# adaLN attention and gated FFN on one core: VectorE sums the softmax denominators over eight key tiles instead of two

## The chip, the core and the metric

The kernel runs on one core of a Trainium2 chip. Five engines work side by side, each through its own instruction stream in order: TensorE (PE, with its weight loads shown as PEld), VectorE (DVE), ScalarE (ACT), GpSimd (POOL) and SyncE (SP), whose only work here is issuing DMA transfers. They wait for each other through semaphores. The metric is the device time of one execution in microseconds (us); the kernel before takes 1217.15 us, the median of three runs from 1216.24 to 1217.86.

## The reference

`x` has 2048 tokens of width 1024. Six modulation vectors come from `silu(c) @ w_mod`. Then, in bf16:

```
h = layernorm(x) * (1 + ca) + sa
q = h @ wq (32 heads of 32);  k = h @ wk, v = h @ wv (one shared head of 32)
p = softmax(q k^T / sqrt(32));  o = p @ v;  x = x + ga * (o @ wo)
h = layernorm(x) * (1 + cb) + sb
x = x + gb * ((silu(h @ w1) * (h @ w3)) @ w2)          # inner width 3584
```

The softmax needs, for each query and head, the sum of its 2048 exponentials. How those sums are made is the core of the change.

## The kernel before

**Tiling.** Queries go in 8 blocks of 256 tokens (`n`). The 32 heads go in 8 groups of 4 (`f`); a block and a group are a *unit* (64 units). A unit runs over 2048 keys in 8 *cycles* (`j`) of two key tiles of 128 keys. So there are 512 cycles.

**One cycle** (`s_exp`): eight score matmuls S (four heads side by side in the array's 32-row strips) write two pairs of the six score banks of PSUM. ScalarE takes two exponentials of 128x1024 from them into `U[c % 10]`. VectorE then adds the two key tiles of the cycle (`pair`, 128x1024, bf16) into `PS[c % 8]`.

**The end of a unit** (`av`): after the unit's last exponential, TensorE runs eight value groups A (eight matmuls each, `V` against `U`, into the left half of one PSUM bank), and after every second one a denominator group M: `ONES` against two of the pair sums `PS`, eight matmuls, into the right half of the same bank. That is four M groups in a unit, 256 in the kernel. Then VectorE normalises: a 32x32 transpose of the right half into `RB[:,0]`, a reciprocal of eight columns, a transpose back into `RB[:,1]`, and a multiply of the bank's left half by it into `QT`. The bank is held until that multiply.

**The rest of a block**: `wo` (output projection, added to `X1` on VectorE, layer norm, transposes), `slab` (14 FFN slabs: gate into one bank, up into another; VectorE halves the gate, ScalarE takes a tanh, VectorE combines, then multiplies with the up bank), `quarter` (four quarters of the down projection; VectorE scales with `GBR`, POOL adds to `X1`). The FFN of block n runs in between the attention of block n+1; the last one runs alone at the end. W1, W3 and W2 are read again for each block, through three slab buffers and two quarter buffers, by SP.

**Banks.** Six of the eight PSUM banks belong to the scores; only two (`PB`) are left for all value, projection and FFN work until the last exponentials are done.

**What sets the order.** A planner (`Placer`) writes each engine's stream at build time. It is a list scheduler: each operation has a duration that the code states, and a `vt` (a due time in cycles). On each engine the operation that can start first goes first, and among those that can start about then the one with the lowest `vt`. On TensorE, S has the lowest (`TOP + c`), then A and M (`-500 + u`), then FFN and projections; a change of the array's mode costs `SWITCH`, and a change between A and F work soon after an S is put off (`HOLD`). On VectorE pair sums have `c + 100`, behind everything else. A TensorE operation of the planner is a group of matmuls that is not split: four in `slab`, `wo` and `q_proj`, seven in `quarter`. `emit` adds the semaphore waits; a VectorE instruction waits for an earlier VectorE instruction only where it reads or overwrites what that one wrote.

All instructions are issued through one helper (`play`, line 22), so the profile names them by tile, not by line. `PB<-PS,ONES` are the M groups, `PB<-U,V` the A groups, `S<-QT,KT` the scores, `PB<-QT,W` and `PB<-QT,HT` the slabs, `PB<-W2S,HT` the quarters. `HT` names all FFN intermediates, which lie in the space of `HT`.

Of the kernel before, what the change touches and what calls it, by code (L numbers as in the profile page):

```python
# [111 lines left out]
class Placer:  # L112

    SWITCH = 0.098
# [114 lines left out]
    def commit(self, n, e, k, start):  # L229
# [11 lines left out]
        if e == "sp" or n.dma is not None:  # L241
            self.t[e] = start + dur
            self.bw = max(self.bw, start + 1.6) + n.nbytes / n.bw
            n.fin = self.bw + 0.5
        else:
            self.t[e] = start + dur
            n.fin = start + dur + n.post + self.SEM
# [24 lines left out]
    def emit(self, n, e, fn):  # L272
# [8 lines left out]
        for p, strong in sorted(n.preds.items(), key=lambda a: -a[0].i):  # L281
            if p.eng == e and p.dma is None and (e == "pe" or not strong):
                continue
# [68 lines left out]
def build(nc, x_in, wq_in, wk_in, wv_in, wo_in, w1_in, w3_in, w2_in, c_in, wmod_in, out, S, D, F):  # L352
# [164 lines left out]
    def ln_stats(xap, tt, keys, vt):  # L517
        for a in range(2):
            op("dve", lambda a=a: [lambda e: e.bn_stats(ST[:, tt, a, :], xap[:, a * 512:(a + 1) * 512])], 0.64,
               reads=keys, writes=[("ST", tt, a)], vt=vt)  # L520
        op("dve", lambda: [lambda e: e.bn_aggr(MV[:, tt, :], ST[:, tt, :, :].rearrange("p a f -> p (a f)"))], 0.17,
# [6 lines left out]
    def ln_norm(xap, tt, keys, slot, vt):  # L528
        op("dve", lambda: [lambda e: e.tensor_scalar(XN[slot], xap, MV[:, tt, 0:1], RS[:, tt:tt + 1],
                                                     ALU.subtract, ALU.mult)], 0.52,  # L530
           reads=keys + [("MV", tt), ("RS", tt)], writes=[("XN", slot)], vt=vt)

    def lnt1(tt, vt):
# [3 lines left out]
        if tt < 8:  # L537
# [4 lines left out]
                                                      scale=RS[:, tt:tt + 1])], 0.98,  # L542
# [11 lines left out]
        op("pe", tr, 0.95, reads=[("XN", slot), "IDENT"], writes=bk, vt=vt, mode="F", sess=s, post=0.2)  # L554
# [8 lines left out]
        op("act", ev_a, 0.98, reads=bk, writes=hk, vt=vt, sess=s, alts=[("dve", ev_d, 0.72)])  # L563

    def mod_cols(fld):
        s = Sess()
        for h in range(2):
# [4 lines left out]
               writes=[("mod", fld)], vt=-1800, mode="F", sess=s, post=0.2)  # L572
# [20 lines left out]
    def k_bias():  # L593
# [4 lines left out]
           sess=s3, post=0.2)  # L598
# [3 lines left out]
    def v_setup():  # L602
# [5 lines left out]
           0.4, reads=["SABR", ("WKV", 1)], writes=["vbr"], vt=-1290, mode="F", sess=s, post=0.2)  # L608
# [3 lines left out]
    def q_bias(f0, f1, key, vt):  # L612
# [4 lines left out]
           reads=[key, "SAB"], writes=[("qbi", f0)], vt=vt, mode="F", sess=s, post=0.2)  # L617
# [3 lines left out]
    def k_proj(j, vt):  # L621
# [6 lines left out]
           writes=[("k", j)], vt=vt, mode="F", sess=s, post=0.2)  # L628
        op("dve", lambda b: [lambda e: e.tensor_scalar(KT[:, ts], BANK[b][:, 0:256], KBI[:, 0:1], None, ALU.add)],
           0.45, reads=[("k", j), "KBI"], writes=[("KT", j)], vt=vt, sess=s,  # L630
           alts=[("act", lambda b: [lambda e: e.activation(KT[:, ts], BANK[b][:, 0:256], ACT.Identity,
                                                           bias=KBI[:, 0:1])], 0.45)])

    def v_proj(tb, vt):
        s = Sess()
        hk = [("HT", cc, tt) for cc in range(NC) for tt in range(4 * tb, 4 * tb + 4)]
        for k in range(4):
# [4 lines left out]
               mode="F", sess=s, post=0.2)  # L642
        op("dve", lambda b: [lambda e: e.tensor_tensor(
            V[:, 4 * tb:4 * tb + 4, :], BANK[b][:, 0:128].rearrange("p (k d) -> p k d", d=32),
            VBR[:].unsqueeze(1).broadcast_to([P, 4, 32]), ALU.add)], 0.3, reads=[("v", tb), "VBR"],
           writes=[("V", tb)], vt=vt, sess=s)

    def q_proj(n, nn, f, vt, cold=1.0):
# [6 lines left out]
        for h in range(2):  # L655
# [3 lines left out]
                for cc in range(4 * h, 4 * h + 4)], pe_mm(w, 4) * cold, reads=wk + hk, writes=[("q", n, f)], vt=vt,  # L659
               mode="F", sess=s, post=0.2)  # L660
        op("dve", lambda b: [lambda e: e.tensor_scalar(
            QT[:, n:n + nn, f, :], BANK[b][:, 0:w].rearrange("p (a t) -> p a t", a=nn), QBI[:, f:f + 1], None,
            ALU.add)], 0.2 + 0.28 * nn, reads=[("q", n, f), ("QBI", f)],
# [4 lines left out]
    def mod_chunk(i, vt):  # L668
# [3 lines left out]
        if i == 1:  # L672
# [7 lines left out]
           writes=[("mc", i)], vt=vt, mode="F", sess=s, post=0.2)  # L680
        if fld in (2, 5):
            op("dve", lambda b: [lambda e: e.tensor_copy(MG[:], BANK[b][:, 0:4])], 0.17, reads=[("mc", i)],
               writes=["MG"], vt=vt, sess=s)
            for k in range(4):
# [5 lines left out]
               reads=["ONES", ("XN", 1)], writes=[("mct", i)], vt=vt, mode="F", sess=s2, post=0.2)  # L690
# [15 lines left out]
    def s_exp(c):  # L706
# [9 lines left out]
        op("pe", mm, 0.225, reads=[("KT", j), ("QT", n, f)], writes=bk, vt=TOP + c, mode="S", post=0.18)  # L716
        for i in range(2):
            def ex(i=i):
# [3 lines left out]
            exps[(c, i)] = op("act", ex, 0.93, reads=[("S", 2 * r[i]), ("S", 2 * r[i] + 1)],  # L722
                              writes=[("U", c % NU, i)], vt=c, post=0.09)

    def pair(c):
        op("dve", lambda: [lambda e: e.tensor_tensor(PS[:, c % NP], U[:, c % NU, :, 0, :], U[:, c % NU, :, 1, :],
                                                     ALU.add)], 0.64,
           reads=[("U", c % NU, 0), ("U", c % NU, 1)], writes=[("PS", c % NP)], vt=c + 100.0)

    def av(u):  # L730
        n, f = u // NC, u % NC
        s = Sess(False)
        for q in range(NP):
            pair(u * NJ + q)
        for q in range(NJ):
            def mm(b, q=q):
# [5 lines left out]
               writes=[("av", u)], vt=-500 + u, mode="A", sess=s, post=0.2, after=[exps[(u * NJ + LAG, 1)]])  # L742
            if q % 2:
                def md(b, q=q):
                    return [lambda e, h=h, k=k: e.matmul(
                        BANK[b][32 * h:32 * (h + 1), B:2 * B], ONES[:, 0:32], PS[:, (u * NJ + k) % NP, h, :],
                        start=False, stop=(k == NJ - 1), tile_position=(0, 32 * h), skip_group_check=True)
                        for k in (q - 1, q) for h in range(4)]
                op("pe", md, 0.22, reads=["ONES"] + [("PS", (u * NJ + k) % NP) for k in (q - 1, q)],
                   writes=[("av", u)], vt=-500 + u, mode="A", sess=s, post=0.2)  # L750
                for k in (q + NP - 1, q + NP):
                    if k < NJ:
                        pair(u * NJ + k)
        vt = u * 8.0
        op("dve", lambda b: [lambda e: e.transpose(RB[:, 0, :], BANK[b][:, B:2 * B])], 0.4, reads=[("av", u)],
           writes=["RBD"], vt=vt, sess=s)
        op("dve", lambda: [lambda e: e.reciprocal(RC[:], RB[:, 0, :].rearrange("p (a r) -> p a r", r=32)[:, :, 0])],
           0.2, reads=["RBD"], writes=["RC"], vt=vt)
        op("dve", lambda: [lambda e: e.transpose(RB[:, 1, :].rearrange("p (a r) -> p a r", r=32),
                                                 RC[:].unsqueeze(2).broadcast_to([P, 8, 32]))], 0.4,  # L760
           reads=["RC"], writes=["RBN"], vt=vt)
        op("dve", lambda b: [lambda e: e.tensor_tensor(QT[:, n, f, :], BANK[b][:, 0:B], RB[:, 1, :], ALU.mult)], 0.42,
           reads=[("av", u), "RBN"], writes=[("QT", n, f)], vt=vt, sess=s)
# [10 lines left out]
    def wo(n, vt):  # L774
        for t in range(2):
            for h in range(2):
                s = Sess()
                for q in range(2):
                    op("pe", lambda b, q=q, h=h, t=t: [lambda e, f=f: e.matmul(
                        BANK[b], QT[:, n, f, t * P:(t + 1) * P], WO[:, f, h * 512:(h + 1) * 512], start=(f == 0),  # L780
                        stop=(f == NC - 1)) for f in range(4 * q, 4 * q + 4)], pe_mm(512, 4),
                       reads=[("QT", n, f) for f in range(4 * q, 4 * q + 4)] + [("WOG", f) for f in
                                                                                 range(4 * q, 4 * q + 4)],
                       writes=[("wo", n, t, h)], vt=vt, mode="F", sess=s, post=0.2)
                xs = X1[:, n % NX, t, h * 512:(h + 1) * 512]
                k = xk(n, t, (2 * h, 2 * h + 1))
                op("dve", lambda b, xs=xs: [lambda e: e.tensor_tensor(xs, xs, BANK[b], ALU.add)], 0.7,
# [3 lines left out]
        for hh in range(2):  # L791
# [4 lines left out]
               writes=[("h2", n, hh)], vt=vt, mode="F", sess=s, post=0.2)  # L796
            for k in range(4):
# [3 lines left out]
                    ALU.mult, ALU.add)], 0.42,  # L801
# [17 lines left out]
    def slab(n, s, vt):  # L819
# [4 lines left out]
        for m in range(2):  # L824
            for sub in range(2):
                for c0 in (0, 4):
                    op("pe", lambda b, m=m, sub=sub, c0=c0: [lambda e, cc=cc: e.matmul(
                        BANK[b][:, sub * B:(sub + 1) * B], W13SL[r][:, m, cc, sub * P:(sub + 1) * P],
                        h2t(n)[:, cc, :], start=(cc == 0), stop=(cc == NC - 1)) for cc in range(c0, c0 + 4)],
                       pe_mm(B, 4), reads=[("W13", r, m)] + h2k(n)[c0:c0 + 4], writes=[("gu", m, n, s)],  # L830
                       vt=vt + 0.01 * m, mode="F", sess=ss[m], post=0.2)
            if m == 0:
                op("dve", lambda b: [lambda e: e.tensor_scalar(GP[:, g, :], BANK[b], 0.5, None, ALU.mult)], 0.72,
# [163 lines left out]
```

## Time and profile before

| what | value |
|---|---|
| median of three runs | 1217.15 us |
| the profiled execution: span from first to last instruction | 1212.5 us |
| TensorE, matmul busy | 1156.9 us (95%) |
| TensorE, weight loads busy | 802.0 us (66%) |
| ScalarE busy | 1042.9 us (86%) |
| VectorE busy | 823.4 us (68%) |
| POOL busy | 95.6 us (8%) |
| first exponential of block 0, of block 4, of block 5 | at 30.1, 572.2, 705.6 us |
| last exponential | at 1104.5 us |
| mean granted TensorE clock | 0.989 |

Of the execution's own time only the span is known; the median lies 4.65 us above it, which is launch and end. From about 218 us to about 1105 us the trace repeats with each block (133.3 us in blocks 3 to 6); before that lie loading, the first layer norm and the projections of block 0, behind it the last FFN. A group's duration in the profile runs until its results have landed; two instructions back to back on one engine overlap by some 0.1 us, so the distance between their starts is the cost, and is read from the timeline.

### The profile page before, as it was taken

What the parts mean: (1) busy time and instruction counts of PE and PEld (TensorE: products, weight loads), DVE (VectorE), ACT (ScalarE), POOL (GpSimd) and SP (SyncE); (2) the same over time, 40 slices, a digit from 0 to 9 for tenths busy, and PEclk for the clock granted to TensorE, in tenths of its full rate; (3) what the DMA queues carried; (4) which work ended last, traced back from release to release, by engine and by line L of the source; (5) the groups of instructions that cost most, each with busy time, mean ns of one, the idle gap of its engine ahead of it and who ended that gap; (6) DMA issues with size and microseconds to landing.
All of it is one profiled execution on the core that took longest, in us unless ns stands there. A gap on an engine that the chain in (4) does not pass through costs nothing.

```text
span 1212.5 us, 37621 instructions
## 1 busy us (share of the span) xinstructions
PE 1156.9 (95%) x17064; PEld 802.0 (66%) x17064; DVE 823.4 (68%) x1456; ACT 1042.9 (86%) x1157; POOL 95.6 (8%) x122
## 2 busy tenths in 40 slices
PE   5898968999999999999999999999999999999997
PEld 5644534777677766677667767676667767676886
DVE  6878757776677757775767657775777667775551
ACT  5698999999999998999999999999899999994110
POOL 5115000000100011001100010001100010001000
PEclk9999988999999999999999999999999999999999
DMA  9422550665486646775396548665486557664995
GB/s 348 144 71 72 153 144 28 183 182 160 124 234 176 176 124 188 197 203 149 97 252 185 148 129 242 180 185 157 122 239 183 151 137 218 178 172 123 280 242 139
DMA packets 367999, 206.50 MB, mean 170 GB/s; under 512 B 5856, under 2 KB 359392, under 8 KB 367840
## 3 DMA queue, kind: packets, MB, share of 16 engines
q1 hardware_dynamic: 367408, 203.97, 60.3%
q8 instruction: 134, 2.20, 0.8%
q14 instruction: 25, 0.20, 0.1%
q10 hardware_dynamic: 432, 0.13, 0.0%
HBM read 199.89 MB, written 4.19 MB: 168 GB/s over the span
## 4 chain that ended last, share of the span: by engine, by line
PE 81%; ACT 10%; DVE 4%; DMA 3%; SPq 1%; issue 0%
PE PB L22 63%; PE S L22 18%; ACT U L22 10%; DVE PS L22 1%; DMA W2S<-in_A_x_dram 1%; DVE ST L22 1%; SPq L22 1%; DVE HT L22 1%; DMA W2S<-in_B_w_dram 1%; DMA W<-in_B_w_dram 1%; DMA HT<-in_B_w_dram 1%; DVE QT L22 0%; DVE RB L22 0%; DVE RC L22 0%; DVE XNB L22 0%
## 5 line engine op out<-in xcount | busy, mean ns | idle before, releaser
L22 ACT ACTIVATE U<-S 128x1024 bf16<-128x1024 f32 x1024 | 973.5, 1034 | 56.1 <-PE S L22 31.4
L22 DVE TENSOR_TENSOR PS<-U 128x1024 bf16<-128x1024 bf16 x512 | 360.8, 708 | 156.3 <-ACT U L22 111.6
L22 PE MATMUL PB<-QT,W 128*128 128x256 bf16 x1856 | 230.1, 273 | 2.0 <-DVE HT L22 2.0
L22 PE MATMUL S<-QT,KT 32*128 32x256 bf16 x4096 | 205.1, 275 | 21.8 <-ACT U L22 19.5
L22 PEld LDWEIGHTS PB<-QT,W 128*128 128x128 bf16 x1856 | 170.1, 98 | 49.2 <-issue 27.8
L22 PE MATMUL PB<-W2S,HT 128*128 128x256 bf16 x1568 | 193.0, 273 | 2.3 <-DMA W2S<-in_B_w_dram 2.3
L22 PEld LDWEIGHTS PB<-W2S,HT 128*128 128x128 bf16 x1568 | 144.7, 98 | 41.8 <-issue 20.5
L22 PE MATMUL PB<-U,V 128*32 128x256 bf16 x4096 | 162.7, 276 | 2.8 <-ACT U L22 1.7
L22 PEld LDWEIGHTS S<-QT,KT 32*128 32x128 bf16 x4096 | 60.9, 92 | 146.4 <-ACT U L22 72.9
L22 ACT ACTIVATE HT<-HT 128x512 bf16<-128x512 bf16 x112 | 70.4, 628 | 66.2 <-DVE HT L22 66.2
L22 PEld LDWEIGHTS PB<-U,V 128*32 128x32 bf16 x4096 | 99.7, 97 | 30.9 <-issue 21.6
L22 PE MATMUL PB<-QT,HT 128*128 128x256 bf16 x928 | 116.9, 273 | 1.0 <-DVE HT L22 1.0
L22 DVE SCALAR_TENSOR_TENSOR HT<-HT 128x512 bf16<-128x512 bf16 x112 | 77.5, 692 | 55.7 <-ACT HT L22 54.7
L22 PE MATMUL PB<-HT,W 128*128 128x256 bf16 (+1 forms) x568 | 101.1, 324 | 2.8 <-DVE QT L22 2.8
L22 PE MATMUL PB<-PS,ONES 128*32 128x256 bf16 x2048 | 101.7, 275 | 0.3 <-issue 0.3
L22 PEld LDWEIGHTS PB<-QT,HT 128*128 128x128 bf16 x928 | 84.8, 98 | 25.0 <-issue 13.9
L22 POOL TENSOR_TENSOR X<-X,HT 128x512 bf16<-128x512 bf16 x28 | 38.4, 1371 | 787.6 <-DVE HT L22 787.6
L22 DVE TENSOR_SCALAR HT<-PB 128x512 bf16<-128x512 f32 x101 | 69.5, 688 | 44.2 <-PE PB L22 42.9
L22 PEld LDWEIGHTS PB<-HT,W 128*128 128x128 bf16 x568 | 51.5, 99 | 38.2 <-issue 8.9
L22 DVE TENSOR_TENSOR HT<-HT,PB 128x512 bf16<-128x512 bf16 x101 | 69.3, 686 | 10.0
L22 PEld LDWEIGHTS PB<-PS,ONES 128*32 128x32 bf16 x2048 | 53.3, 97 | 6.5 <-issue 5.2
L22 PE MATMUL PB<-WO,QT 128*128 128x512 bf16 x224 | 55.0, 380 | 0.0
(97 smaller groups left out, 652.0 us busy)
## 6 DMA issues: line engine op xcount, KB each, us to landing
W<-in_B_w_dram SPq DMA_DIRECT2D x150, 512.0 KB, 4.8
W2S<-in_B_w_dram SPq DMA_DIRECT2D x32, 1792.0 KB, 8.8
HT<-in_B_w_dram SPq DMA_DIRECT2D x74, 512.0 KB, 4.8
W2S<-in_w_mod_dram SPq DMA_DIRECT2D x8, 1024.0 KB, 5.4
X<-in_A_x_dram SPq DMA_DIRECT2D x8, 512.0 KB, 5.0
U<-in_w_mod_dram SPq DMA_DIRECT2D x4, 1024.0 KB, 8.9
out_dram<-X SPq DMA_DIRECT2D x8, 512.0 KB, 8.0
W2S<-in_A_x_dram SPq DMA_DIRECT2D x2, 1024.0 KB, 14.5
```

Source lines behind the costliest of these rows:

```text
L22: return getattr(e, call[0])(*call[1], **call[2])
```

## The change

- **Sums over eight key tiles.** The pair sums are made for two cycles by one instruction (128x2048, `pairs`). Further VectorE adds (128x1024, in place in `PS`) join them two and two, and these again: each unit has 4 wide adds and 6 further adds where it had 8 adds. `PS[0]` and `PS[4]` then hold the sums over eight key tiles each, and one M group per unit, behind the last A group, reads these two.
- **The bank is copied out.** After the transpose, VectorE copies the left half of the bank to `RB[:,1]`; the transpose back goes to `RB[:,0]`, and the multiply reads SBUF only. The bank is free after the copy.
- **Shorter groups.** `slab`, `wo`, `q_proj` and `quarter` hand the planner groups of two matmuls.
- **POOL's adds.** The scaling of `WO` with the gate (8 instructions) and the FFN's adds to `X1` (28, for blocks 0 to 6) go to VectorE.
- **Waits.** VectorE now also waits for an earlier VectorE instruction that reads what it is to overwrite.
- **The planner's numbers.** Most stated durations, the latency behind a TensorE group (`post`, 0.2 to 0.145), `SWITCH` and the DMA latency are changed. They act on the order alone.

```
-            if p.eng == e and p.dma is None and (e == "pe" or not strong):
+            if p.eng == e and p.dma is None and (e == "pe" or (e != "dve" and not strong)):
...
-    def pair(c):
-        op("dve", lambda: [lambda e: e.tensor_tensor(PS[:, c % NP], U[:, c % NU, :, 0, :], U[:, c % NU, :, 1, :],
-                                                     ALU.add)], 0.64,
-           reads=[("U", c % NU, 0), ("U", c % NU, 1)], writes=[("PS", c % NP)], vt=c + 100.0)
+    def pairs(c):
+        m = c % NU
+        op("dve", lambda: [lambda e: e.tensor_tensor(PS[:, c % NP:c % NP + 2], U[:, m:m + 2, :, 0, :],
+                                                     U[:, m:m + 2, :, 1, :], ALU.add)], 1.12,
+           reads=[("U", m + k, i) for k in range(2) for i in range(2)],
+           writes=[("PS", (c + k) % NP) for k in range(2)], vt=c + 101.0, post=0.08)
...
-        for q in range(NP):
-            pair(u * NJ + q)
+        for q in range(0, NP, 2):
+            pairs(u * NJ + q)
+            for w in (1, 2):
+                if (q + 2) % (2 * w) == 0:
+                    k0 = q + 2 - 2 * w
+                    k1 = q + 2 - w
+                    op("dve", lambda k0=k0, k1=k1: [lambda e: e.tensor_tensor(PS[:, k0], PS[:, k0], PS[:, k1], ALU.add)],
+                       0.602, reads=[("PS", k0), ("PS", k1)], writes=[("PS", k0)], vt=u * NJ + q + 102.0)
...
-            if q % 2:
+            ks = [0, 4] if q == NJ - 1 else []
+            if ks:
...
+        op("dve", lambda b: [lambda e: e.tensor_copy(RB[:, 1, :], BANK[b][:, 0:B])], 0.31, reads=[("av", u)],
+           writes=["AVS"], vt=vt, sess=s)
...
-        op("dve", lambda b: [lambda e: e.tensor_tensor(QT[:, n, f, :], BANK[b][:, 0:B], RB[:, 1, :], ALU.mult)], 0.42,
-           reads=[("av", u), "RBN"], writes=[("QT", n, f)], vt=vt, sess=s)
+        op("dve", lambda: [lambda e: e.tensor_tensor(QT[:, n, f, :], RB[:, 1, :], RB[:, 0, :], ALU.mult)], 0.36,
+           reads=["AVS", "RBD"], writes=[("QT", n, f)], vt=vt)
...
-                for c0 in (0, 4):
+                for c0 in range(0, NC, 2):
...
-            for f0 in range(0, NF, 7):
+            for f0 in range(0, NF, 2):
...
-        eng, d = ("dve", 0.36) if n == NB - 1 else ("pool", 1.1)
-        op(eng, lambda: [lambda e: e.tensor_tensor(xs, xs, O2B[:, q % 2], ALU.add)], d,
+        op("dve", lambda: [lambda e: e.tensor_tensor(xs, xs, O2B[:, q % 2], ALU.add)], 0.34,
...
-        op("pool", lambda f=f: [lambda e: e.tensor_tensor(WO[:, f, :], WO[:, f, :], GAR[:], ALU.mult)], 2.2,
+        op("dve", lambda f=f: [lambda e: e.tensor_tensor(WO[:, f, :], WO[:, f, :], GAR[:], ALU.mult)], 0.605,
```

116 lines of the change are left out of this document (56 added, 60 removed).

## The prediction

> **What bounds the kernel now.** I read four views in this order: the busy shares of the page, the same shares by stretches of time, the TensorE timeline of one block, and the groups and waits of that block.
>
> ```profile
> PE 1156.9 (95%) x17064; PEld 802.0 (66%) x17064; DVE 823.4 (68%) x1456; ACT 1042.9 (86%) x1157; POOL 95.6 (8%) x122
> ...
> 30.00:176.00 146.00, 129.07 (x2029) 70.09 (x2027) 109.92 (x199) 126.15 (x136) 25.12 (x21) 0.95 0.41 122
> ...
> 572.20:705.50 133.30, 131.59 (x2000) 91.77 (x2000) 92.73 (x163) 127.50 (x143) 7.57 (x8) 1.00 0.64 175
> ...
> 1105.50:1212.50 107.00, 97.32 (x928) 81.87 (x928) 46.48 (x78) 8.86 (x15) 5.41 (x7) 0.99 0.79 205
> ```
>
> The columns behind the length of a stretch are the busy time of PE, weight loads, DVE, ACT and POOL, then the clock, the DMA share and GB/s. In a block of the steady part (the third line) TensorE stands still for 133.3 - 131.6 = 1.7 us, ScalarE for 5.8, VectorE for 40.6. TensorE is the bound there, ScalarE close behind, and VectorE is the engine with room. In block 0 (second line) nobody is full; behind 1105 us ScalarE has nearly nothing to do.
>
> ```profile
> 571.79 0.40 PE L22 MATMUL S<-QT,KT 32*128 32x256 bf16 x8
> 572.26 0.62 PE L22 MATMUL PB<-U,V 128*32 128x256 bf16 x16
> 572.71 0.39 PE L22 MATMUL PB<-PS,ONES 128*32 128x256 bf16 x8
> 572.93 0.61 PE L22 MATMUL PB<-U,V 128*32 128x256 bf16 x16
> ```
>
> One group follows the other with no gap, and the M group of line three costs 572.93 - 572.71 = 0.22 us of TensorE's time.
>
> ```profile
> L22 DVE TENSOR_TENSOR PS<-U 128x1024 bf16<-128x1024 bf16 x64 | 43.6, 685 | 20.3 <-ACT U L22 13.6 <-PE PB L22 6.6
> L22 PE MATMUL PB<-PS,ONES 128*32 128x256 bf16 x256 | 12.6, 273 | 0.0
> L22 DVE TENSOR_TENSOR HT<-HT,PB 128x512 bf16<-128x512 bf16 x14 | 9.6, 687 | 1.4
> ...
> 628.49 1.29 DVE L22 TENSOR_TENSOR PS<-U 128x1024 bf16<-128x1024 bf16 x2 [1.16 <-PE PB L22]
> ...
> 630.89 0.45 DVE L22 STREAM_TRANSPOSE RB<-PB 128x256 f32<-128x256 f32 x1 [0.18 <-PE PB L22]
> 631.38 0.20 DVE L22 RECIPROCAL RC<-RB 128x8 f32<-128x8 f32 x1
> ```
>
> The first group says that half of VectorE's idle time in a block (20.3 of 40.6 us) lies before pair sums; the other 20.3 us lie before work that frees PSUM banks. From the fourth line, two adds of 0.69 us take 1.29 us together, so one costs 1.29 - 0.69 = 0.60 us when the next is ready. By the last two lines a dependent one starts after 0.49 us, where transposes that nobody waits for are 0.37 us apart: waiting for one's own engine costs about 0.11 us.
>
> **The change, part by part**, for one steady block (8 units, 64 cycles).
>
> *M groups.* 32 become 8: 24 x 0.22 = 5.3 us less on TensorE. Its work falls from 131.6 to 126.3 us.
>
> *Sums on VectorE.* Removed: 64 x 0.605 = 38.7 us. Added: 32 wide adds. No row has that width; from 0.34 us at 512 elements (X<-X,HT lasts 0.424 us, less the overlap of 0.085) and 0.605 at 1024 it is 0.605 + 1024 x 0.265/512 = 1.14 us, and at most 2 x 0.605 = 1.21. That is 36.5 us. 48 further adds x 0.605 = 29.0 us. Together +26.8 us. Each further add waits for the add before it: 0 where other work lies between, 48 x 0.11 = 5.3 us where none does. The rows above show that wait, 0.49 against 0.37 us, so I keep both ends. The Trainium skill, page VectorE: DVE Perf Modes, section The DRAIN you can't avoid, holds that a semaphore between two VectorE instructions costs nothing extra; by it the 5.3 us would be zero.
>
> *Copy of the value half.* +8 x 0.34 = 2.7 us, priced by the multiply of the same size (QT<-PB,RB, starts 0.34 us apart); the multiply itself stays. It changes when the bank comes free. Now it is held from the first A group to the multiply's end: the M groups end 3.2 us behind the first A, the multiply 5.4. Afterwards transpose and copy are 0.37 + 0.34 us, so 1.4 us per unit are gained at that end. At the other end the last sums come later: behind the unit's last exponential a wide add and two further ones must run, 1.14 + 2 x 0.605 + 3 x 0.11 = 2.7 us, where one add of 0.6 sufficed. The A groups and a score group fill 8 x 0.22 + 0.5 = 2.3 us of that. M waits at the head of TensorE's stream, with the next S behind it and through S the exponentials; so lateness of the sums beyond some 0.4 us costs TensorE directly unless the planner puts FFN groups ahead of M. Likewise the next unit's first wide add must wait for this M, which reads `PS[0]`; it is due two cycles (about 4 us) behind the last exponential, and bank readers stand behind it on VectorE.
>
> *POOL's adds.* X adds: 4 x 0.34 = 1.4 us on VectorE per block, instead of 1.34 us each on POOL; the output transfer behind them on SP leaves a microsecond earlier, and nobody waits for it. The `WO` scaling: 8 x 0.605 = 4.8 us, once, at about 86 us, where VectorE is busy for 78% of the time; hidden, since the first output projection is one block away; 4.8 us if it is not. No transfer is moved.
>
> *Shorter groups.* Sixteen slab matmuls in four groups run at 109 ns from start to start already (1.91 us for 16), so a border between groups costs TensorE nothing. Scores come sooner: ScalarE waits for TensorE 4.7 us in a block. With TensorE full this only moves FFN work later, so 0; at best a part of the 1.7 us.
>
> *The new self-waits.* Buffers rewritten at once are rare: 0, at most 0.11 us for a few. *Planner's numbers*: no row prices an order; between -1.7 us (all idle time gone) and the loss worked out next.
>
> *What gets worse.* VectorE's work in a block, start to start: before 38.7 + 8 x 1.2 (normalising) + 36.4 (FFN: 42 slab operations and 12 others x 0.605, 12 small ones 3.7) = 84.7; afterwards 36.5 + 29.0 + 12.3 + 37.8 = 115.6, or 120.9 with all self-waits. That is 89 to 93% of the time. A bank reader that becomes ready meets an add under way: 38.7/133 x 0.3 us before, (36.5 x 0.57 + 29.0 x 0.3)/130 afterwards, 0.09 against 0.23, so 0.14 us more for each of 52 bank readers (28 in the slabs, 8 in the other groups, 8 behind transposes, 8 normalising): 7.3 us, if no second bank were free. The value bank is held for 5.4 - 1.4 = 4.0 of some 16.5 us, so I charge a quarter, 1.8 us. TensorE's idle time goes from 1.7 to 3.5 us (ends: 1.7 and 9.0).
>
> *Sum.* A block takes 126.3 + 3.5 = 129.8, 3.5 us less; seven blocks: -24.5. VectorE allows that if half of its 20.3 us of unfilled waiting remains: 118.2 + 10.2 = 128.4. ScalarE allows it too, since 5.8 us of its idle time are there to lose. Block 0 is bound by turns by loading, ScalarE and projections: 0, between -5.3 (24 M groups) and +5 (VectorE gets 28 + 4.8 us more to do on 110 of 146). The end: 3 M groups less, -0.7, against FFN work that ran late and now meets the DMA, which is 79% busy there: together 0, ends -0.7 and +4. Total -24: span 1212.5 to 1188.5, and with the 4.65 us by which the median lies above it 1193 us.
>
> **The rivals.**
>
> *VectorE becomes the bound, and the kernel slower.* The place is the steady block. If VectorE's 20.3 us of waiting before bank readers cannot be filled, since a gap of 0.4 us holds no add of 1.14, a block lasts 118.2 + 20.3 = 138.5 us: 5.2 x 7 = +36, 1254 us. It decides once more than 15 of the 20.3 us remain. For it: the streams are in order, and all three engines would stand above 89%. Against it: the adds may be placed as fillers and are ready long before they are needed.
>
> *TensorE is not the bound.* The Perfetto Trace Analysis page of the Trainium skill (Identifying the Most-Contended Engine) says that matmul busy time is a bad measure and weight-load busy time a good one. That is 91.8 of 133.3 us, 69%, in the block shown. As a mechanism: the chain of exponentials (127.5 of 133.3 us) sets the pace, TensorE's 5.3 us turn into idle time, and with VectorE's delays nothing is won: 1217 us. Against it, the timeline shows group after group without a gap, and the chain of waits has 81% of the span on TensorE. By that page's rule the time would stay; by the rows it falls.
>
> *All of it is won.* TensorE's idle time stays at 1.7 us, block 0 wins a part: 7 x 5.3 + 3 = -40, 1177 us. For it: ScalarE's floor is lower still (exponentials start 0.90 us apart where they are ready: 128 x 0.90 + 14 x 0.52 = 122.5 us).
>
> **How the numbers follow.** Forecast (1193 us, own range 1178 to 1209) 0.62; all won 0.12; TensorE not the bound 0.06; VectorE the bound (1222 to 1260) 0.20. Faster by over 0.2% (about what a measurement of this kernel can tell from no change) is 0.62 + 0.12 = 0.74, within it 0.06, slower 0.20. The predicted time is the likeliest case's. The range from 1171 to 1228 leaves out some 0.04 of the fast and 0.15 of the slow case.
>
> **What would show it.** M groups: 64 x 8 matmuls, 42 us of TensorE's busy time gone. Wide adds 1.14 us apart (1.22 long). Steady blocks of about 130 us with VectorE above 90% busy and TensorE idle for 3 to 4 us. Normalising multiply off the bank. If the VectorE rival holds, TensorE's waits for DVE (0.5 us in the block now) grow past 8 us, and ScalarE's waits for scores with them. I would be wrong by size if block 0 or the end moved by over 5 us, or if the order alone freed or cost ScalarE more than its 5.8 us.

## The result, and the profile after

The changed kernel takes **1196.19 us** in the median of four runs, against 1216.70 for four runs of the kernel before in the same measurement (1217.15 in the three named above): a ratio of 0.9825, with a 95% interval from 0.9807 to 0.9843. The forecast was 1193. The profiled execution spans 1194.0 us, 18.5 less than before, at a mean granted clock of 0.991 (before 0.989).

The 4.65 us by which the median before lies above its profiled span are not all launch and end: wherever time and span of one execution are both known they lie 1.75 to 2.19 us apart (1195.81 and 1194.0 for the profiled one of the changed kernel). The rest, some 2.8 us, says that the profiled execution of the kernel before was a quick one.

First the page's busy shares and the engines of its chain of waits, after:

```profile
PE 1122.4 (94%) x15493; PEld 756.5 (63%) x15528; DVE 1011.7 (85%) x1681; ACT 1024.1 (86%) x1160; POOL 39.1 (3%) x86
...
PE 49%; ACT 33%; DVE 12%; DMA 3%; issue 1%; POOL 1%; SPq 0%
```

TensorE had 81% of the chain before and has 49% now: the end is now reached through TensorE, ScalarE and VectorE by turns. The same shares by stretches of time, after. The columns are as in the prediction; the lines are block 0, blocks 1 to 7, the end behind the last exponential, and two steady blocks.

```profile
30.60:172.40 141.80, 124.65 (x1854) 64.22 (x1872) 124.61 (x226) 124.75 (x138) 4.82 (x12) 0.98 0.34 104
172.40:1072.50 900.10, 869.24 (x12408) 582.57 (x12424) 815.33 (x1320) 875.33 (x995) 16.76 (x28) 0.99 0.63 174
1072.50:1194.00 121.50, 110.34 (x1016) 93.77 (x1016) 52.85 (x90) 9.27 (x15) 1.70 (x4) 0.98 0.78 203
...
683.00:812.70 129.70, 126.97 (x1810) 86.14 (x1810) 117.42 (x191) 125.19 (x143) 1.58 (x4) 1.00 0.66 180
812.70:942.70 130.00, 127.04 (x1809) 86.02 (x1809) 117.46 (x192) 125.06 (x143) 1.96 (x4) 1.00 0.66 180
```

And before, cut at the same places (first exponential, last of block 0, last of all):

```profile
30.10:175.80 145.70, 128.97 (x2027) 69.99 (x2025) 109.82 (x199) 125.85 (x136) 25.02 (x21) 0.96 0.41 122
175.80:1105.50 929.70, 912.77 (x13880) 633.79 (x13880) 647.83 (x1132) 892.53 (x995) 49.36 (x53) 0.99 0.61 168
1105.50:1212.50 107.00, 97.32 (x928) 81.87 (x928) 46.48 (x78) 8.86 (x15) 5.41 (x7) 0.99 0.79 205
```

Three things are to be seen. Blocks 1 to 7 became 29.6 us shorter and block 0 3.9 us. The end became 14.5 us longer. And in blocks 1 to 7 TensorE now stands still for 900.1 - 869.2 = 30.9 us, where it was 16.9: part of its saved work has turned into idle time. By single blocks, 5 to 7 became 3.3 to 3.6 us shorter and block 1 3.5; blocks 2 to 4 became 2.0, 6.1 and 7.6 us shorter, and there some 118 matmuls less are recorded than the M groups account for: work of other kinds that was put off.

The longer end holds work that used to lie in the blocks. Its matmul count less the last unit's A and M matmuls gives the FFN and projection matmuls (F) behind the last exponential: 928 - 64 - 32 = 832 before, 1016 - 64 - 8 = 944 after. 112 more of them at 0.109 us from start to start are 12.2 us; TensorE's idle time there rose by another 1.5 us (9.7 to 11.2). Its longest piece is a wait for weights, in TensorE's timeline after:

```profile
1118.66 1.91 PE L22 MATMUL S<-QT,HT 128*128 128x256 bf16 x16
1123.90 2.47 PE L22 MATMUL PB<-QT,HT 128*128 128x256 bf16 x16 [3.34 <-DMA HT<-in_B_w_dram]
```

The groups of the page, after, answer to the three shown of before (a line from the listing by form is the third):

```profile
L22 DVE TENSOR_TENSOR PS<-U 128x2048 bf16<-128x2048 bf16 x256 | 307.7, 1206 | 9.8 <-ACT U L22 9.1
L22 DVE TENSOR_TENSOR PS<-PS 128x1024 bf16<-128x1024 bf16 x384 | 259.8, 681 | 3.5
...
L22 PE MATMUL PB<-PS,ONES 128*32 128x256 bf16 x504 | 25.1, 277 | 1.1 <-DVE PS L22 0.9
```

M has fallen from 2048 to 512 matmuls (504 in this line; the last unit's eight write to a bank of the scores and have a line of their own), and VectorE waits 9.8 us ahead of its wide adds in the whole run, where one block held 20.3 us ahead of its pair sums.

### The profile page after: what moved, and what is told of

The parts are those of the page before. It is cut to its first block, busy times and chain, and to the rows that moved or that the text cites. A ratio compares the mean times of both kernels' runs of the same rounds, so it can differ in the third digit from the quotient of the medians.

```text
span 1194.0 us, 34630 instructions
## 1 busy us (share of the span) xinstructions
PE 1122.4 (94%) x15493; PEld 756.5 (63%) x15528; DVE 1011.7 (85%) x1681; ACT 1024.1 (86%) x1160; POOL 39.1 (3%) x86
## 4 chain that ended last, share of the span: by engine, by line
PE 49%; ACT 33%; DVE 12%; DMA 3%; issue 1%; POOL 1%; SPq 0%
PE PB L22 37%; ACT U L22 31%; PE S L22 13%; DVE PS L22 6%; DVE HT L22 2%; ACT HT L22 2%; DMA W2S<-in_B_w_dram 2%; DVE RB L22 1%; DVE QT L22 1%; DMA HT<-in_B_w_dram 1%; DMA U<-in_w_mod_dram 1%; POOL RS L22 1%; DVE X L22 1%; DVE ST L22 0%; POOL PS L22 0%
## 5 line engine op out<-in xcount | busy, mean ns | idle before, releaser
L22 DVE TENSOR_TENSOR PS<-U 128x2048 bf16<-128x2048 bf16 x256 | 307.7, 1206 | 9.8 <-ACT U L22 9.1
L22 DVE TENSOR_TENSOR PS<-PS 128x1024 bf16<-128x1024 bf16 x384 | 259.8, 681 | 3.5
L22 PE MATMUL PB<-QT,W 128*128 128x256 bf16 x1856 | 232.7, 273 | 4.4 <-DVE HT L22 3.6
L22 PE MATMUL PB<-W2S,HT 128*128 128x256 bf16 x1456 | 184.1, 273 | 1.2 <-DMA W2S<-in_B_w_dram 0.9
L22 PEld LDWEIGHTS PB<-W2S,HT 128*128 128x128 bf16 x1456 | 132.2, 98 | 44.7 <-issue 24.7
L22 ACT ACTIVATE HT<-HT 128x512 bf16<-128x512 bf16 x112 | 83.4, 744 | 88.1 <-DVE HT L22 88.1
L22 PE MATMUL PB<-U,V 128*32 128x256 bf16 x4032 | 131.8, 276 | 3.3 <-ACT U L22 1.3
L22 PEld LDWEIGHTS PB<-U,V 128*32 128x32 bf16 x4032 | 97.9, 97 | 30.4 <-issue 18.5
L22 PEld LDWEIGHTS PB<-HT,W 128*128 128x128 bf16 x568 | 50.0, 99 | 45.1 <-issue 15.6
L22 DVE STREAM_TRANSPOSE RB<-PB 128x256 f32<-128x256 f32 x63 | 28.3, 449 | 56.4 <-PE PB L22 56.4
L22 POOL TENSOR_SCALAR RS<-MV 128x1 f32<-128x1 f32 x32 | 11.8, 370 | 1041.4 <-DVE MV L22 1040.8
```

The source lines that it names most:

```text
L22: return getattr(e, call[0])(*call[1], **call[2])
```

## Experiments

Ratios are to the kernel before, run beside each (medians from 1216.70 to 1217.28 us), with their 95% interval. "Hold" is the time from a unit's first A group to the instruction that frees its `PB` bank, averaged over units 8 to 55 of the trace: 5.80 us before, 3.98 after (forecast 5.4 and 4.0). "Idle" is TensorE's idle time in blocks 1 to 7.

| kernel | median us | ratio, interval | idle us | F behind the last exponential |
|---|---|---|---|---|
| before | 1217.15 | 1 | 16.9 | 832 |
| after | 1196.19 | 0.9825 [0.9807, 0.9843] | 30.9 | 944 |
| before + sums | 1251.09 | 1.0273 [1.0249, 1.0298] | 73.0 | 1224 |
| before + short groups | 1226.77 | 1.0064 [1.0040, 1.0088] | 26.4 | 922 |
| before + POOL's adds moved | 1220.50 | 1.0029 [1.0019, 1.0039] | 28.4 | 849 |
| before, M thinned | 1228.69 | 1.0093 [1.0075, 1.0112] | 55.3 | 731 |
| after - sums | 1205.23 | 0.9909 [0.9890, 0.9928] | 17.0 | 1121 |
| after - copy | 1249.30 | 1.0271 [1.0251, 1.0291] | 71.6 | 1271 |
| after, adds back on POOL | 1222.72 | 1.0038 [1.0022, 1.0054] | 36.8 | 919 |
| after, long groups | 1201.89 | 0.9865 [0.9843, 0.9886] | 35.4 | 776 |
| after, numbers of before | 1204.86 | 0.9897 [0.9878, 0.9917] | 41.6 | 911 |
| after - further adds | 1180.57 | 0.9691 [0.9673, 0.9710] | 22.9 | 924 |
| after, paced | 1224.76 | 1.0069 [1.0050, 1.0088] | 52.5 | 776 |
| after, one number | 1194.88 | 0.9820 [0.9800, 0.9839] | 31.5 | 945 |

Four of the twelve expectations below held the measured time in a range that they named (adds back on POOL, further adds left out, long groups, one number). In the other eight the time lies outside every range given, so these runs show sizes that none of the theories foretold.

### The sums alone, in the kernel before

```
-        for q in range(NP):
-            pair(u * NJ + q)
+        for q in range(0, NP, 2):
+            pairs(u * NJ + q)
+            for w in (1, 2):
...
-            if q % 2:
+            ks = [0, 4] if q == NJ - 1 else []
+            if ks:
```

> The kernel before with the sums over eight key tiles alone (wide pair adds, running adds, one denominator group per unit); groups, bank, POOL's adds and the planner's other numbers stay. Theory T (the denominator groups taken from TensorE are the gain; what the attention phase wins is partly given back behind the last exponential, since scores go first and FFN work is left over): about 1198 us, 1190 to 1208, steady blocks of 125 to 130 us, and a longer end, by 30 us or more, since the stream holds some 400 more FFN matmuls behind the last score group than before. Rival U (the shorter groups are the gain, and the sums alone only load VectorE): 1215 to 1235 us.

1251.09 us: 34 us slower than before. The step from which the prediction took all of its gain, put alone, loses more than it was to win. Idle rises from 16.9 to 73.0 us, 1224 F matmuls are left behind the last exponential, and the hold grows from 5.80 to 7.48 us. The step is thus worth nothing by itself here; the next runs say what else it needs.

### The copy taken out of the changed kernel

```
-        op("dve", lambda b: [lambda e: e.tensor_copy(RB[:, 1, :], BANK[b][:, 0:B])], 0.31, reads=[("av", u)],
-           writes=["AVS"], vt=vt, sess=s)
...
-        op("dve", lambda: [lambda e: e.tensor_tensor(QT[:, n, f, :], RB[:, 1, :], RB[:, 0, :], ALU.mult)], 0.36,
+        op("dve", lambda b: [lambda e: e.tensor_tensor(QT[:, n, f, :], BANK[b][:, 0:B], RB[:, 1, :], ALU.mult)], 0.36,
```

> The kernel after without the copy of the value half: the multiply reads the bank, as before, and the bank is held for some 1.4 us more per unit, while VectorE has 2.5 us less to do per block. Theory C (the early release of the bank is what makes the sums pay; the sums alone, where the bank was held to the multiply, came out at 1251 us): 1205 to 1225 us. Theory N (the planner's numbers do that): 1194 to 1200 us.

1249.30 us: 53 us worse than the changed kernel, for one instruction of 0.31 us per unit. The hold is 7.17 us instead of 3.98. VectorE's timeline of the run without the copy shows why:

```profile
613.69 0.45 DVE L22 STREAM_TRANSPOSE RB<-PB 128x256 f32<-128x256 f32 x1 [3.70 <-PE PB L22]
614.06 1.18 DVE L22 TENSOR_TENSOR PS<-U 128x2048 bf16<-128x2048 bf16 x1
615.16 0.19 DVE L22 RECIPROCAL RC<-RB 128x8 f32<-128x8 f32 x1
615.28 0.69 DVE L22 TENSOR_TENSOR PS<-PS 128x1024 bf16<-128x1024 bf16 x1
615.89 0.68 DVE L22 TENSOR_TENSOR HT<-PB,GBR 128x512 bf16<-128x512 f32 x1
616.49 0.43 DVE L22 STREAM_TRANSPOSE RB<-RC 128x256 f32<-128x256 f32 x1
616.85 0.38 DVE L22 TENSOR_TENSOR X<-X,HT 128x512 bf16<-128x512 bf16 x1
617.15 0.41 DVE L22 TENSOR_TENSOR QT<-PB,RB 128x256 bf16<-128x256 f32 x1
```

and the same place of a unit in the changed kernel:

```profile
706.56 0.45 DVE L22 STREAM_TRANSPOSE RB<-PB 128x256 f32<-128x256 f32 x1 [0.29 <-PE PB L22]
706.93 0.39 DVE L22 COPY RB<-PB 128x256 f32<-128x256 f32 x1
707.24 0.18 DVE L22 RECIPROCAL RC<-RB 128x8 f32<-128x8 f32 x1
707.34 1.17 DVE L22 TENSOR_TENSOR PS<-U 128x2048 bf16<-128x2048 bf16 x1
...
709.82 0.42 DVE L22 TENSOR_TENSOR QT<-RB 128x256 bf16<-128x256 f32 x1
```

The epilogue has four dependent instructions, and VectorE, busy for 786.6 of 920.6 us in blocks 1 to 7 of this run, has adds between them. From transpose to multiply pass 3.46 us without the copy and 3.26 us with it; what differs is that with the copy the bank has been free since 707.3. TensorE's waits in blocks 1 to 7 of the run without the copy say it from the other side (engine, tile, awaited; total us, times, longest):

```profile
PE S L22 <- ACT U L22: 33.5, 44, 1.4
...
PE PB L22 <- DVE HT L22: 17.5, 37, 1.1
...
PE PB L22 <- DVE RC L22: 13.4, 15, 1.2
```

Its waits for VectorE to free a bank (the last two lines) add up to 30.9 us; the changed kernel has 5.7 us on the first of the two, and 1.7 us on `RB`, which the copy writes, in place of the second. Its waits for exponentials, the first line, are 15.6 us in the changed kernel. Of the 56 us of span, 20.5 lie in blocks 1 to 7 and 35.9 in the end, where 327 more F matmuls than in the changed kernel are 35.6 us: the scores go first, so what TensorE loses in the blocks falls on the FFN and comes back behind the last exponential.

### POOL's adds put back in the changed kernel

```
-        op("dve", lambda: [lambda e: e.tensor_tensor(xs, xs, O2B[:, q % 2], ALU.add)], 0.34,
+        eng, d = ("dve", 0.34) if n == NB - 1 else ("pool", 1.35)
+        op(eng, lambda: [lambda e: e.tensor_tensor(xs, xs, O2B[:, q % 2], ALU.add)], d,
...
-        op("dve", lambda f=f: [lambda e: e.tensor_tensor(WO[:, f, :], WO[:, f, :], GAR[:], ALU.mult)], 0.605,
+        op("pool", lambda f=f: [lambda e: e.tensor_tensor(WO[:, f, :], WO[:, f, :], GAR[:], ALU.mult)], 2.5,
```

> The kernel after with the 28 adds to X1 and the 8 scalings of WO on POOL, as before, at the durations that the profile shows (1.35 and 2.5 us). VectorE has 1.4 us less to do per block and 4.8 us once. By the forecast these adds are hidden wherever they are: 1192 to 1198 us. If VectorE's load is what limits after (its 230 us of running adds cost 16 us in all): the 14 us less would win about 1 us. If POOL's slower adds were in the way of the sums alone: 1205 us or more.

1222.72 us: the whole gain is gone, and 5.6 us more, although VectorE has 9.5 + 4.8 us less to do (28 adds of 0.34, 8 of 0.605). VectorE's timeline of this run, beside the `WO` scaling on POOL:

```profile
94.28 3.14 DVE L22 TENSOR_TENSOR PS<-U 128x2048 bf16<-128x2048 bf16 x1
97.35 0.74 DVE L22 TENSOR_SCALAR QT<-PB,QBI 128x512 bf16<-128x512 f32 x1
98.01 1.94 DVE L22 TENSOR_TENSOR PS<-PS 128x1024 bf16<-128x1024 bf16 x1
```

its POOL timeline, and TensorE's wait behind a sum:

```profile
91.58 21.52 POOL L22 TENSOR_TENSOR WO<-WO,XNB 128x1024 bf16<-128x1024 bf16 x8 [48.03 <-DVE XNB L22]
...
114.42 0.40 PE L22 MATMUL PB<-PS,ONES 128*32 128x256 bf16 x8 [3.96 <-DVE PS L22]
```

A wide add takes 3.14 us instead of 1.2, a further add 1.94 instead of 0.69; the addition that reads PSUM between them takes its usual 0.74. So VectorE's sums and POOL's instructions, each with both inputs in SBUF, take turns. Over the whole run, the sums that overlap one of these POOL instructions are longer by 27.6 us in total than the median of the others, 13.2 of it in block 0; block 0 is 15.1 us longer (156.9 against 141.8) and blocks 1 to 7 13.3 us. The kernel before had it too, with 11.0 us, all of it on eight pair sums beside the `WO` scaling in block 0, and a group's mean hardly shows that: 708 ns over all 512 pair sums, 685 in the block shown ahead. In its VectorE timeline, two pair sums that otherwise take 1.29 us together:

```profile
94.18 5.08 DVE L22 TENSOR_TENSOR PS<-U 128x1024 bf16<-128x1024 bf16 x2
```

The Trainium skill, page SBUF — State Buffer, section SBUF: two separate sides, says that VectorE and GpSimd share a pair of ports under an exclusive lock, held for the whole instruction, when the VectorE instruction has two SBUF inputs and GpSimd's reads SBUF, while the other blocks fully. The trace agrees: 3.14 against 1.2 us, and the PSUM reader untouched.

### POOL's adds moved alone, in the kernel before

```
-        eng, d = ("dve", 0.36) if n == NB - 1 else ("pool", 1.1)
-        op(eng, lambda: [lambda e: e.tensor_tensor(xs, xs, O2B[:, q % 2], ALU.add)], d,
+        d = 0.36
+        op("dve", lambda: [lambda e: e.tensor_tensor(xs, xs, O2B[:, q % 2], ALU.add)], d,
...
-        op("pool", lambda f=f: [lambda e: e.tensor_tensor(WO[:, f, :], WO[:, f, :], GAR[:], ALU.mult)], 2.2,
+        op("dve", lambda f=f: [lambda e: e.tensor_tensor(WO[:, f, :], WO[:, f, :], GAR[:], ALU.mult)], 0.7,
```

> The kernel before with POOL's adds (28 to X1, 8 scalings of WO) moved to VectorE alone. In the trace of before 35 pair sums that ran beside a POOL add were stretched, by 11 us in all; where VectorE is loaded with sums (the run with the adds back on POOL) 45 adds were stretched by 28 us, and the kernel was 26 us slower. Theory P (the stretch only costs where VectorE is near full): 1211 to 1219 us here. Rival (it costs in any case): 1198 to 1208 us.

1220.50 us, 0.3% slower: where VectorE has 40 us of room per block, moving the adds wins nothing in the whole. By place it is not nothing. Block 0 and blocks 1 to 7 of this run:

```profile
30.00:171.40 141.40, 125.49 (x2011) 69.14 (x2026) 103.85 (x207) 125.47 (x136) 5.21 (x13) 0.96 0.42 126
171.40:1109.80 938.40, 909.97 (x13850) 633.40 (x13865) 653.35 (x1156) 891.63 (x995) 15.60 (x28) 0.99 0.60 166
```

Block 0, where the stretched sums lay, is 4.3 us shorter (141.4 against 145.7). Blocks 1 to 7 are 8.7 us longer; why was not traced. The same edit is worth 26.5 us beside the sums: it is a condition of them.

### All but the sums

The changed kernel with the pair sums and four M groups per unit of before.

```
-    def pairs(c):
+    def pair(c):
...
-        for q in range(0, NP, 2):
-            pairs(u * NJ + q)
-            for w in (1, 2):
+        for q in range(NP):
+            pair(u * NJ + q)
...
-            ks = [0, 4] if q == NJ - 1 else []
-            if ks:
+            if q % 2:
```

> The kernel after without the sums over eight key tiles: 8 pair adds and 4 denominator groups per unit as before; bank copy, short groups, adds on VectorE and the planner's new numbers stay. Theory S (the 42 us of denominator groups are the gain, once the early bank release and the move of POOL's adds make room for them): 1210 to 1230 us, steady blocks some 5 us longer than after's 128.6. Rival R (the other steps are the gain, and the sums only move work): 1185 to 1198 us.

1205.23 us. The steps that the prediction priced at nothing (copy, short groups, POOL's adds, numbers) give 11.9 of the 21 us; the sums on top of them give 9.0, of 192 x 0.22 = 42 us that they take off TensorE. The stretches of this run, block 0, blocks 1 to 7 and the end:

```profile
30.30:166.70 136.40, 125.05 (x2023) 68.94 (x2037) 103.51 (x212) 125.11 (x138) 5.14 (x12) 1.00 0.37 113
166.70:1061.10 894.40, 877.36 (x13574) 603.95 (x13592) 648.80 (x1193) 871.62 (x989) 15.80 (x28) 1.00 0.61 168
1061.10:1202.90 141.80, 131.45 (x1217) 112.78 (x1216) 60.31 (x102) 12.59 (x20) 1.58 (x4) 0.97 0.83 216
```

Attention is over 44 us earlier than before (1061.1 against 1105.5), and the end is 35 us longer, with 1121 F matmuls instead of 832. What remains of the gain lies in block 0: 136.4 us against 145.7, 9.3 of the 9.6 us between the two spans. From here to the changed kernel the end loses 20.3 us (177 fewer F matmuls are 19.3), while block 0 grows by 5.4 and blocks 1 to 7 by 5.7 us. So the sums win 14.6 us in the blocks and the end together and lose 5.4 in block 0. The time freed of M was filled with FFN work that had been put off, and idle time took 13.9 us of it (17.0 to 30.9).

### The further adds left out

```
-            for w in (1, 2):
+            for w in ():
```

> The kernel after without the six further adds of each unit (384 x 0.6 = 230 us of VectorE's time); the denominators are then sums over four of the sixteen key tiles, so this leaves out part of the computation. It prices VectorE's load with TensorE's work unchanged. Theory T: VectorE costs TensorE some 1 to 2 us a block, so 1180 to 1192 us. Rival V (VectorE is the bound of after): 1160 to 1178 us. If VectorE's load costs nothing: 1194 to 1198 us.

1180.57 us, 15.6 less than the changed kernel. 384 x 0.60 = 230 us of VectorE's work cost 15.6 us of time. With them VectorE is busy for 815.3 of 900.1 us in blocks 1 to 7 (91%), without them for 70%, and TensorE's idle time falls from 30.9 to 22.9 us. VectorE is near enough to full to be felt, and does not set the pace alone.

### M thinned in the kernel before

Nothing but the last M group of each unit is issued.

```
+                if q == NJ - 1:
-                op("pe", md, 0.22, reads=["ONES"] + [("PS", (u * NJ + k) % NP) for k in (q - 1, q)],
+                    op("pe", md, 0.22, reads=["ONES"] + [("PS", (u * NJ + k) % NP) for k in (q - 1, q)],
```

> The kernel before with three of the four denominator groups of a unit left out and all pair adds kept; the denominators are then sums over the last four key tiles, so this leaves out part of the computation. It takes the same 42 us of work off TensorE as the change does, and puts nothing on VectorE. Theory T (TensorE is the bound of before): 1174 to 1192 us. The rival that TensorE is not the bound: 1210 to 1217 us.

1228.69 us: 42 us of TensorE's work are gone, nothing was added to any engine, and the kernel is 11.5 us slower. Blocks 1 to 7 last 946.6 us with 55.3 us of idle time, 38.4 more than before, about what the M groups had taken there (168 x 0.22 = 37.0). TensorE's timeline of this run:

```profile
603.75 0.40 PE L22 MATMUL S<-QT,KT 32*128 32x256 bf16 x8 [0.16 <-ACT U L22]
605.59 0.40 PE L22 MATMUL S<-QT,KT 32*128 32x256 bf16 x8 [1.44 <-ACT U L22]
605.92 1.07 PE L22 MATMUL PB<-IDENT,XNB 128*128 128x128 bf16 x16
607.42 0.40 PE L22 MATMUL S<-QT,KT 32*128 32x256 bf16 x8 [0.44 <-ACT U L22]
609.25 0.40 PE L22 MATMUL S<-QT,KT 32*128 32x256 bf16 x8 [1.44 <-ACT U L22]
```

For a while TensorE has scores to issue and little else, and the scores wait for the exponentials to free their buffers: 42.4 us of such waits in blocks 1 to 7, against 10.8 before. Only 731 F matmuls are left for the end, so F was done sooner. The timeline shows that the planned order has hardly any F at such places; whether some could have stood there, and why the planner comes to this order, was not traced.

### FFN first where it is overdue

```
+        if e == "pe":
+            old = min([n.vt for st, n in cand if n.mode == "F"], default=1e9)
+            cyc = [n.vt + 1e6 for st, n in cand if n.mode == "S"]
+            if cyc and old > 64 and old < cyc[0] - PACE:
+                cand = [c for c in cand if c[1].mode != "S"]
```

> The kernel after with one rule more in the planner: FFN or projection work that is more than six cycles overdue goes ahead of the next scores. The order then leaves 756 instead of 924 FFN matmuls behind the last score group. Theory D (the longer end is work that was put off, and no loss by itself): the end 15 to 20 us shorter than after's 121.5, the blocks together as much longer, total 1190 to 1202 us. Rival L (the end loses time to weight transfers, so putting off costs): 1178 to 1188 us.

1224.76 us. The end does become 22 us shorter than in the changed kernel (99.5 us, 776 F matmuls), but blocks 1 to 7 become 53.7 us longer. ScalarE's waits for scores there are 67.9 us in 28 waits, up to 7.6 us each, and TensorE's idle time is 52.5 us. The long end is thus not simply waste, at least not for this rule: the put-off FFN work is what TensorE is filled with elsewhere.

### Groups of two alone, and long groups in the changed kernel

```
-                for c0 in (0, 4):
+                for c0 in range(0, NC, 2):
...
-            for f0 in range(0, NF, 7):
+            for f0 in range(0, NF, 2):
```

> The kernel before with the shorter matmul groups alone. Theory T: TensorE has the same work and was full, so 1213 to 1218 us; ScalarE's waits for scores shrink from 4.7 us a block, and the attention phase and the end trade time. Rival U: 1195 to 1202 us.

1226.77 us in the kernel before, 0.6% slower. The opposite edit in the changed kernel:

> The kernel after with the groups of before (four and seven matmuls). Theory T: 1194 to 1204 us; steady blocks a little longer than after's 128.4 us on average (scores wait for a group's end), the end shorter, since some 150 fewer quarter matmuls are left behind the last score group: about 17 us. Rival U: 1212 to 1220 us.

1201.89 us, 5.7 us worse than the changed kernel. In the two kernels the same step goes opposite ways; whether what stands around it or the order that came out decides that is open (see the next section).

### The planner's numbers of before, and one number alone

The stated durations and `post` go back to those of before, with the changed structure kept; those of the sums and of the normalising stay as in the changed kernel.

```
-    SWITCH = 0.1
+    SWITCH = 0.098
...
-                   writes=[("av", u)], vt=-500 + u, mode="A", sess=s, post=0.145)
+                   writes=[("av", u)], vt=-500 + u, mode="A", sess=s, post=0.2)
```

> All the steps of the kernel after (sums, bank copy, shorter groups, adds on VectorE, self-waits) with the planner's durations, latencies, mode cost and DMA latency of the kernel before. Theory N (with three engines near full, an order planned with wrong durations leaves TensorE waiting): 1215 to 1250 us, TensorE idle for 5 us or more in a steady block. Theory C (the copy makes the sums pay): 1194 to 1202 us.

1204.86 us, 8.7 us worse than the changed kernel. The second run asks how much of such a difference is chance of the order: it changes nothing but the first of these numbers.

> A control: the kernel after with one planner number, the cost of a mode change, put back from 0.1 to 0.098. The operations are the same, their order differs in many places. It tells how far the time moves by the order alone: within 3 us of after (1193 to 1199) if the order is sound in general, 5 to 15 us off if the time hangs on details of one order; differences of that size between the other runs would then say nothing on their edits.

1194.88 us, 1.3 us from the changed kernel and within its interval. The control is weaker than it was meant to be. By the two traces VectorE's instructions come in the same order except in blocks 3 to 5, and TensorE's differ by more than a few matmuls only there; the other edits change far more of the order. So it does not tell how far a wholly different order moves the time, and no such control was run for the kernel before. The steps of 53 and 26 us have a mechanism that the traces show (the held bank, the stretched sums). For the smaller ones, the 15.6, 11.9 and 9.0 us among them, and for the 9.6 and 11.5 us that two edits cost the kernel before, no run separates the edit from the order that the planner made of it.

## Why the prediction was right, and where it was not

The time lies 3.2 us above the forecast and inside both ranges. That it came so near is in part luck: errors in the sum went against each other, and more than half of the gain came from steps that it priced at nothing. Its terms, against what the profiled execution shows:

| place | forecast us | measured us |
|---|---|---|
| block 0 | 0 (-5.3 to +5) | -3.9 |
| blocks 1 to 7 | -24.5 | -29.6 |
| end | 0 (-0.7 to +4) | +14.5 |
| span, with +0.5 ahead of block 0 | -24 | -18.5 |

In spans the forecast was thus 5.5 us off (1188.5, measured 1194.0). The 3.2 us between the medians are fewer because 4.65 us were added for launch and end, where the median after lies 2.2 above its span: a third error, and a lucky one.

**Block 0: the sum near, its parts not.** The -3.9 us are -9.3 from the other steps and +5.4 from the sums, as the run without the sums shows. The forecast had the second (its bound of +5, VectorE's new load) and not the first.

**The steady block: right where nothing else moved.** Blocks 1 and 5 to 7 are 3.3 to 3.6 us shorter each (forecast 3.5), with TensorE idle for 2.2 to 3.0 us in blocks 5 to 7 (3.5). Blocks 2 to 4 are 15.7 us shorter in all, but about 12.9 of that is the 118 put-off matmuls, nearly all of which come back at the end.

**The end: mis-sized, and outside its bounds.** By over 5 us it is what the prediction named as a sign of being wrong by size. I looked there only at 3 M groups and the DMA. What moved is the border: 112 F matmuls (12.2 us) now lie behind the last exponential. The rule that scores go first was in my own text: if attention gets faster and FFN does not, FFN falls behind. "With TensorE full this only moves FFN work later, so 0" was the very place to price it.

**"24 x 0.22 = 5.3 us less on TensorE": right in size, wrong in worth.** The M groups went as said. But the 42 us are worth 9.0 us beside the other steps, and less than nothing without them (1251.09, and 1228.69 with M merely thinned). In blocks 1 to 7 the books read: M -37.0 us; 112 fewer F matmuls -12.2, as many as the end has more (counted by weight loads, 13880 - 12424 - 1344, since 16 matmuls lack a record); idle time +13.9 (forecast 12.6); sum -35.3 against -29.6 measured. About 6 us of longer matmul work I cannot place.

**Copy, POOL's adds, groups and numbers at 0: wrong, together 11.9 us without the sums.** Nearly all of it lies in block 0; which of the four gives how much of it was not run. The copy's time was right (hold 5.80 to 3.98 us, forecast 5.4 to 4.0), but I priced it against the kernel before; beside the sums the alternative is 7.17 us, since wide adds slip into the epilogue. It is worth 53 us there. "Hidden" for POOL's adds missed that on POOL they stop VectorE's sums: 26.5 us. Each of the two looked like a small cost for a small gain, and without either the gain is gone.

**VectorE's load: its prices right, its sum not quite comparable.** The wide add starts the next instruction after 1.09 to 1.14 us (forecast 1.14), the copy after 0.31 (0.34), and blocks 5 to 7 last 129.7 to 130.0 us (129.8). VectorE is busy for 117.4 us of a steady block, within the 115.6 to 120.9 of the forecast; but that sum is of starts and gave 84.7 before, where the profile has 92.7 busy. By the profile's measure the load grew by 24.7 us, not by 31 to 36.

**The rivals.** VectorE as the bound did not come about in the changed kernel, but something near it did where the copy is missing or POOL's adds remain: the kernel is slower than before (1249 and 1223 us). Without the copy VectorE is busy for 85% of blocks 1 to 7 only; it is late there, not full. I gave it 0.20 without seeing that two small edits decide it. "All of it is won" did not come, since idle time rose. "TensorE is not the bound" I put at 0.06, because the timeline shows no gap. The thinned M groups show that this argument does not carry by itself: a stretch with no gap says that there was work to fill with, and in the order that the planner made, less of it did not make the stretch shorter. On this point the Perfetto Trace Analysis page of the Trainium skill (Identifying the Most-Contended Engine), which mistrusts matmul busy time, was nearer than my reading: 42 us less of it gave +11.5 us, though by its rule as I used it the time would have stayed. ScalarE's row tells where the gain could come from. Exponentials, before:

```profile
L22 ACT ACTIVATE U<-S 128x1024 bf16<-128x1024 f32 x1024 | 973.5, 1034 | 56.1 <-PE S L22 31.4 <-PE PB L22 16.8
```

and after:

```profile
L22 ACT ACTIVATE U<-S 128x1024 bf16<-128x1024 f32 x1024 | 967.1, 1131 | 34.0 <-PE PB L22 16.6 <-PE S L22 16.3
```

The third part is ScalarE's idle time ahead of exponentials: 56.1 to 34.0 us, 15.1 of the 22.1 in waits for scores (31.4 to 16.3). Without the sums it is 30.7 us already. The 22 us are about the gain of the whole change, though the two need not be the same time.

**What stays open.** Why thinner M groups and short groups alone make the kernel before slower was seen as idle time and waits, not followed to a choice of the planner. The effects of groups and numbers, and the split of the gain into 11.9 and 9.0 us, are not separated from the order. A version that beats the changed kernel and computes all of it did not come out.

## What to carry to other kernels

Where three engines stand near 90% and a planner fills the gaps, work removed from the fullest engine need not be a saving by itself; here it became one only once a bank came free sooner and a slower partner stood out of the way. So price a step against the kernel that has the other steps, not against the one before. Ask of every dependent chain on the engine that gets the new work how long it holds a bank once foreign instructions fall between its links. And where one kind of work goes first, count what it leaves behind its last instruction.

## What the hardware showed

- **VectorE and POOL stop each other** when VectorE's bf16 sums and POOL's add or scaling both take two inputs from SBUF: 1024 columns 0.69 to 1.9 us and more (up to 2.60), 2048 columns 1.2 to 3.14 us, while VectorE's PSUM readers (0.74 us) and transposes (0.45 us) kept their durations. POOL waits as well: eight `WO` instructions take from 2.23 to 3.10 us each.
- **A VectorE instruction that needs the one before it costs about 0.13 us.** In the trace after, one further add starts 0.71 to 0.73 us behind another in 54 places and 0.60 in 22. A dependent pair, where two independent ones take 1.29 us:

```profile
693.26 1.42 DVE L22 TENSOR_TENSOR PS<-PS 128x1024 bf16<-128x1024 bf16 x2
```

The section The DRAIN you can't avoid (the Trainium skill, page VectorE: DVE Perf Modes), weighed in the prediction, finds no extra cost for a semaphore after each of eight copies. By this row a dependent add has one, of the size of the 0.11 us that I kept as an end.
